# Softmax attention beside linear attention on one core: a new order for all five engines, and 76 of VectorE's score groups that add their second exponential pattern by an accumulating transfer

## The chip, the cores and the metric

The kernel runs on one core of one Trainium2 chip. The metric is the device time of one execution in microseconds (us). The core has five engines with queues of their own: TensorE (PE, matmuls into PSUM, which has eight banks of 128 x 512 float32), VectorE (DVE), ScalarE (ACT), GpSimd (POOL) and SyncE (SP, which here issues transfers only). SP, ACT and POOL can each issue transfers (DMAs); the page names such queues SPq, ACTq and POOLq. PEld is the loading of weights into TensorE.

## The reference

The input x has 2048 rows of 512 columns; there are 32 heads of 16. Branch A is linear attention with a softmax feature map, branch B is softmax attention, and a gate mixes the two:

```
g = sigmoid((x * gate_w).sum(-1, keepdims=True))
A:  phi(p) = concat(softmax(p), softmax(-p)),  p = q @ w_phi  or  k @ w_phi
    o = (phi_q @ (phi_k^T v)) / (phi_q . sum(phi_k) + 1e-6);   a = o @ wo
B:  p = softmax(q k^T / 4);   b = (p v) @ wo
return g * a + (1 - g) * b
```

Nearly all the work is in branch B: 32 heads x 2048 x 2048 scores, each of which goes through an exponential.

## The kernel before

**Tiles and units of work.** A tile is a 128 x 512 block of scores: 128 keys of one head by 512 queries. Four heads at a time make a quad of four tiles, and there are 512 quads (32 blocks of 16; a block is 8 heads' even or odd half against 512 queries). TensorE writes a tile into one PSUM bank (L892, one matmul that uses 32 rows of the array). Then the exponential is made by one of two engines:

- ScalarE takes 324 quads: one ACTIVATE with Exp reads two tiles, now and then three or one (L975), and writes bf16 into a ring of 24 tiles, E_t. One round of four matmuls (L903) then multiplies the four tiles by the values and adds them into the block's bank of sums.
- VectorE takes 188 quads, called groups: `add_group`. It adds a constant to the scores and writes them as 16-bit integers whose bits, read as bf16, are a coarse exponential (L938; L933 where two tiles go in one instruction, "pairs"). That is the first pattern, in a buffer t. GpSimd adds 35 to each 16-bit number (INT64_ADD on four at a time, L919, operation s) and writes a second buffer s; later it adds 48 more in place (operation m). The three patterns together approximate the exponential. In this kernel each gives a round of four matmuls on TensorE: `ps` (pattern two, from s), `pt` (pattern one, from t) and `pm` (pattern three, from s after m).

A group has a fourth number, `acc`, that is 0 for all of them here. With `acc` 1 the round `ps` is not made; instead GpSimd issues a transfer that adds buffer s onto buffer t in on-chip memory (L948), and `pt` waits for it:

```
if acc:
    op = P.add("pool", lambda e: e.dma_start(quarters(t), quarters(s), accum_op=ALU.add), reads=[s], ...)
else:
    ops.append(add_round(quad, part(s), [s], f"ps.{n}"))
ops.append(add_round(quad, part(t), [(t, i) for i in range(4)], f"pt.{n}"))
ops.append(shifted(n, s, s, STEPS[1] - STEPS[0], "m"))
ops.append(add_round(quad, part(s), [s], f"pm.{n}"))
```

A buffer is 128 x 2048 bf16, 512 KB. Operation m writes s, so it waits for that transfer too. The buffers are a pool of tiles that are free in that stage of the program: Tx_t, Ty_t, Tz_t, WoA_t, WoB_t, oT_t and phiQT_t from the start, WAT_t, vA_t, Wp_t and WB_t once the weights in them are used up.

**Small transfers.** When a block's sums are complete, its division goes over a chain of small DMAs on SP: Tf_t to memory (ld, L1018), back in another shape (Lq, L1020), VectorE's reciprocal, out (lr, L1027), back as a broadcast (Rb_t, eight DMAs, L1029), beside a merge of Tf_t (four DMAs, L1023). New queries need two sets of four small DMAs on qz_t (L850, L852).

**Branch A for queries** runs in four steps of 512 queries between the tiles of branch B. ScalarE makes the exponentials EA_t, VectorE scales them, SP writes them to memory (`pw`, L1247, dpq<-EA_t). SP then issues eight transposing transfers back (`Tq`, L1253: four into phiQT_t, four into WAT_t). They wait for the four writes and, for the first step, for the last use of phiQT_t as a group buffer. TensorE's denominators (`Z`, L1265) wait for all eight; numerators (`N`, L1278) follow. EA_t has two halves, so TensorE's projection for a later 128 queries (`P0`, L709) waits for the write of an earlier one.

**What sets the order.** Each engine executes its queue in order, and a waiting instruction holds all behind it. `TABLE` lists, for every engine, the numbers of its operations in the order in which they are issued, besides the split of quads between ScalarE and VectorE (`acts`, `groups`), the tiles of each Exp (`sizes`), the PSUM bank of each fill (`homes`) and the pairs (`pairs`). The semaphore waits are derived from the data that each operation reads and writes. `WENG` names the queue that loads each part of the weights of branch B.

Of the kernel before, what the change touches and what calls it, by code (L numbers as in the profile page):

```python
# [34 lines left out]
WENG = ("sp", "pool", "sp", "sp", "sp", "sp")  # L35
TABLE = {
    "acts": [
# [11 lines left out]
    "sizes": (  # L49
        "32332323322222221222212222222222222222222222222222222222222222222222222222222222222222222222222222332222222222222222222222222222222322222232"  # L50
        "22222222222222222222222222222222222222222222222222223232222222222222222222222222222222222222222222222222222222222222222222222222222222222222"
        "22222222222222222222232322222222222222222222222222222222222222222222222222222222222222222223222221222222222222222222222222222222222222222222"
        "22222222222222222222222222222222222222222222222222222222222222222222222222222222222222222222222222222222222222222222222222222222222222222222"
        "2222222222222222222222222222222222222222222222222222222222222222222222222223132122"),
    "groups": [
# [508 lines left out]
def _build(ctx, nc, A_x, A_wqkv, A_w_phi, A_wo, B_wqkv, B_wo, gate_w, out, table):  # L564
# [81 lines left out]
    for i, (nm, o, n) in enumerate((("wbk0", D, 128), ("wbq0", 0, 128), ("wbv0", 2 * D, 128),  # L646
                                    ("wbq", 128, 384), ("wbk", D + 128, 384), ("wbv", 2 * D + 128, 384))):
        dma(WENG[i], lambda e, o=o, n=n: e.dma_start(W_B[:, :, o:o + n], wb_v[:, :, o:o + n]), [nm], name=nm)
    for rr in range(8):
# [754 lines left out]
```

## Time and profile before

| | |
|---|---|
| median of 2 runs | 695.08 us (695.07 to 695.09) |
| the profiled execution | 696.42 us |
| its span, first to last instruction | 694.6 us |
| mean granted TensorE clock | 0.979 |
| bytes moved by DMAs | 30.93 MB |

The profile is of one execution; its busy times, counts and waits all belong to the 694.6 us. In views by window, each engine's busy time is followed by its number of instructions in brackets, then the granted TensorE clock as a share of full speed, the busy share of the DMA engines and what they moved. In timelines a row gives start and duration in us, the engine, the line and the tiles; in square brackets stands the idle time before it and what ended it.

### The profile page before, as it was taken

What the parts mean: (1) busy time and instruction counts of PE and PEld (TensorE: products, weight loads), DVE (VectorE), ACT (ScalarE), POOL (GpSimd) and SP (SyncE); (2) the same over time, 40 slices, a digit from 0 to 9 for tenths busy, and PEclk for the clock granted to TensorE, in tenths of its full rate; (3) what the DMA queues carried; (4) which work ended last, traced back from release to release, by engine and by line L of the source; (5) the groups of instructions that cost most, each with busy time, mean ns of one, the idle gap of its engine ahead of it and who ended that gap; (6) DMA issues with size and microseconds to landing.
All of it is one profiled execution on the core that took longest, in us unless ns stands there. A gap on an engine that the chain in (4) does not pass through costs nothing.

```text
span 694.6 us, 20402 instructions
## 1 busy us (share of the span) xinstructions
PE 673.4 (97%) x8759; PEld 231.6 (33%) x8759; DVE 627.4 (90%) x955; ACT 645.6 (93%) x713; POOL 408.2 (59%) x418
## 2 busy tenths in 40 slices
PE   7999999999999999999998999999999999999997
PEld 4433334343333342323332332322333323222222
DVE  6898897988988989999996899899999998999996
ACT  3999999999999999999996899899999998999993
POOL 4474534554546536697745567463676636875785
PEclk9999999999999999999997899899999999999999
DMA  9011100101000000010203115231232241111120
GB/s 221 6 37 35 36 21 15 25 3 36 5 11 22 1 20 18 17 52 10 59 18 95 27 37 123 57 89 30 71 88 89 56 97 31 54 36 28 30 43 32
DMA packets 62522, 30.93 MB, mean 45 GB/s; under 512 B 46216, under 2 KB 57352, under 8 KB 62432
## 3 DMA queue, kind: packets, MB, share of 16 engines
q1 hardware_dynamic: 61424, 28.95, 17.2%
q8 instruction: 69, 1.13, 0.7%
q10 hardware_dynamic: 576, 0.52, 0.2%
q0 software_dynamic: 432, 0.15, 0.1%
q14 instruction: 21, 0.17, 0.1%
HBM read 9.44 MB, written 8.88 MB: 26 GB/s over the span
## 4 chain that ended last, share of the span: by engine, by line
PE 73%; DVE 14%; SPq 4%; ACT 3%; DMA 3%; issue 2%; POOL 1%; DVEq 0%
PE ps L892 27%; PE ps L903 26%; PE ps L709 13%; SPq L1253 3%; ACT E_t L975 3%; PE ps L1182 2%; DVE vA_t L938 2%; DVE vA_t L933 1%; PE ps L795 1%; DVE oT_t L1032 1%; PE ps L808 1%; DMA WAT_t<-dpq 1%; DVE Tz_t L938 1%; DVE oT_t L938 1%; PE ps L1278 1%
## 5 line engine op out<-in xcount | busy, mean ns | idle before, releaser
L975 ACT ACTIVATE E_t<-ps 128x1024 bf16<-128x1024 f32 (+1 forms) x642 | 613.8, 1043 | 33.2 <-PE ps L892 29.2
L892 PE MATMUL ps<-qz_t,kTB_t 32*128 32x512 bf16 x2048 | 287.9, 389 | 7.1 <-DVE vA_t L938 1.4
L892 PEld LDWEIGHTS ps<-qz_t,kTB_t 32*128 32x128 bf16 x2048 | 74.5, 91 | 242.4 <-ACT E_t L975 117.9
L903 PE MATMUL ps<-E_t,vaug_t 128*32 128x512 bf16 (+1 forms) x1296 | 122.7, 388 | 0.1
L938 DVE TENSOR_SCALAR oT_t<-ps 128x512 int16<-128x512 f32 x128 | 84.1, 683 | 5.1 <-PE ps L892 4.6
L919 POOL INT64_ADD Tx_t<-Tx_t x45 | 47.2, 1050 | 43.1 <-PE ps L903 43.0
L938 DVE TENSOR_SCALAR vA_t<-ps 128x512 int16<-128x512 f32 x104 | 68.3, 681 | 2.7 <-PE ps L892 2.2
L919 POOL INT64_ADD vA_t<-vA_t x49 | 51.2, 1048 | 29.3 <-PE ps L903 16.5
L919 POOL INT64_ADD Ty_t<-Ty_t x42 | 43.6, 1040 | 22.5 <-PE ps L903 18.1
L903 PEld LDWEIGHTS ps<-E_t,vaug_t 128*32 128x32 bf16 (+1 forms) x1296 | 32.1, 95 | 47.4 <-issue 38.6
L938 DVE TENSOR_SCALAR phiQT_t<-ps 128x512 int16<-128x512 f32 x60 | 40.6, 686 | 5.9 <-PE ps L892 5.4
L709 PE MATMUL ps<-Wp_t,xT_t 128*32 128x512 bf16 x512 | 42.5, 390 | 3.1 <-DMA dpq<-EA_t 3.0
L903 PE MATMUL ps<-vA_t,vaug_t 128*32 128x512 bf16 x464 | 45.1, 389 | 0.4 <-POOL vA_t L919 0.4
L903 PE MATMUL ps<-Ty_t,vaug_t 128*32 128x512 bf16 x388 | 38.6, 390 | 0.4 <-POOL Ty_t L919 0.4
L903 PE MATMUL ps<-Tx_t,vaug_t 128*32 128x512 bf16 x388 | 38.4, 391 | 0.0
L709 PE MATMUL ps<-xT_t,WB_t 128*32 128x512 bf16 x480 | 37.5, 383 | 0.6 <-DVE Ty_t L933 0.6
L938 DVE TENSOR_SCALAR WoB_t<-ps 128x512 int16<-128x512 f32 x50 | 33.0, 684 | 5.0 <-PE ps L892 4.5
L938 DVE TENSOR_SCALAR WoA_t<-ps 128x512 int16<-128x512 f32 x52 | 34.4, 685 | 3.0 <-PE ps L892 2.7
L938 DVE TENSOR_SCALAR Ty_t<-ps 128x512 int16<-128x512 f32 x50 | 33.0, 681 | 1.8 <-PE ps L892 1.5
L938 DVE TENSOR_SCALAR Wp_t<-ps 128x512 int16<-128x512 f32 x46 | 30.3, 684 | 2.5 <-PE ps L892 2.0
L933 DVE TENSOR_SCALAR vA_t<-ps 128x1024 int16<-128x1024 f32 x24 | 29.2, 1221 | 1.6 <-PE ps L892 1.5
L938 DVE TENSOR_SCALAR Tx_t<-ps 128x512 int16<-128x512 f32 x44 | 29.0, 682 | 1.3 <-PE ps L892 1.1
(207 smaller groups left out, 992.6 us busy)
## 6 DMA issues: line engine op xcount, KB each, us to landing
dpq<-EA_t SPq DMA_DIRECT2D x16, 256.0 KB, 2.2
Rb_t<-lr SPq DMA_DIRECT2D x120, 32.0 KB, 1.8
dpo<-kv_t SPq DMA_DIRECT2D x16, 128.0 KB, 1.8
qz_t<-qz_t SPq DMA_DIRECT2D x120, 16.0 KB, 1.8
Tf_t<-Tf_t SPq DMA_DIRECT2D x60, 32.0 KB, 2.0
phiK_t<-in_A_x_dram SPq DMA_DIRECT2D x3, 512.0 KB, 8.0
WB_t<-in_B_wqkv_dram SPq DMA_DIRECT2D x3, 384.0 KB, 4.5
out_dram<-WvA_t SPq DMA_DIRECT2D x8, 128.0 KB, 1.9
```

Of the source, the lines that this page charges most:

```text
L709: ins = e.matmul(out[32 * i:32 * i + 32, :], lhsT=lhsT[:, 32 * i:32 * i + 32], rhs=rhs, start=start, stop=stop, tile_position=(0, 32 * i))
L795: mms = [lambda e, ap, i=i, t=t: e.matmul(ap[:, 128 * i:128 * (i + 1)], lhsT=xT[:, t, NQ * c + 128 * i:NQ * c + 128 * (i + 1)], rhs=W_B[:, ...
L808: mms = [lambda e, ap, i=i, t=t: e.matmul(ap[:, 256 * i:256 * (i + 1)], lhsT=xT[:, t, NQ * c + 128 * (2 * hf + i):NQ * c + 128 * (2 * hf + ...
L892: op = P.add("pe", lambda e: e.matmul(f.ap(), lhsT=kT_B[32 * i:32 * i + 32, ROW[b // 2] % 2, 128 * kt:128 * (kt + 1)], rhs=qz[32 * i:32 * ...
L903: return e.matmul(P.sums[b].ap()[32 * i:32 * i + w, :], lhsT=vaug[:, kt, o:o + w], rhs=rhs, start=start, stop=stop, tile_position=(0, 32 * ...
L919: op = P.add("pool", lambda e: e.int64_add(quarters(dst).bitcast(I64), quarters(src).bitcast(I64), step * 0x0001000100010001), reads=[(src ...
L933: return e.tensor_scalar(quarters(t)[:, a[0]:a[1] + 1:a[1] - a[0], :].bitcast(I16), ps3[:, c[0]:c[1] + 1:c[1] - c[0], :], EXPB, 0.0, op0=A ...
L938: d = P.add("dve", lambda e, i=i, f=f: e.tensor_scalar(quarters(t)[:, group.places.index(i), :].bitcast(I16), f.ap(), EXPB, 0.0, op0=ALU.a ...
L975: return e.activation(Ebuf[:, 512 * k:512 * (k + n)].rearrange("p (a c) -> p a c", c=512), ps3[:, where[0]:where[-1] + 1:step, :], ACTF.Ex ...
L1032: P.add("dve", lambda e: e.tensor_tensor(oT[:, r, qc, :], Tf[:, 0, :], Rb[:], ALU.mult), reads=[("Tf", 0), "Rb"], writes=[("oT", qc, r)], ...
L1182: mms = [lambda e, ap, n=n, f=f: e.matmul(ap[:, 64 * n:64 * n + 64].rearrange("p (s g j) -> p s g j", s=2, j=4), lhsT=ident[:], rhs=es[n][ ...
L1253: turned(f"Tq{n % 2}", [lambda e, g=g: e.dma_start_transpose(qT(g), dpq[n % 2, :, 128 * g:128 * (g + 1)]) for g in range(8)], [("dpq", n % ...
```

## The change

Only numbers change. ScalarE gets 322 quads in place of 324, VectorE 190 groups in place of 188; 76 of these groups (numbers 0 to 3 of every ten) have `acc` 1. So the rounds of four matmuls with the values go from 324 + 3 x 188 = 888 to 322 + 3 x 190 - 76 = 816, and GpSimd issues 76 accumulating transfers of 512 KB. ScalarE's Exp instructions go from 642 (620 of two tiles, 17 of three, 5 of one) to 641 (623, 12, 6); the pairs from 71 to 67. One weight load, 128 KB for the first queries, moves from GpSimd's queue to ScalarE's. The order of all five queues and the banks are new throughout.

```diff
-WENG = ("sp", "pool", "sp", "sp", "sp", "sp")
+WENG = ("sp", "act", "sp", "sp", "sp", "sp")
...
-        (3, "woA", "x0", 0), (19, "woB", "x1", 0), (7, "o2", "y0", 0), (15, "o3", "y1", 0), (14, "pt", "z", 0), (31, "woA", "woB", 0), (30, "o2", "x0", 0),
...
+        (3, "woA", "x0", 1), (19, "woB", "x1", 1), (11, "o2", "y0", 1), (10, "o3", "y1", 1), (15, "pt", "z", 0), (31, "woA", "x0", 0), (30, "pt", "y0", 0),
...
```

Three places are shown as they stand in the engines' queues. Names: ISA is GpSimd's INT64_ADD; a number such as x8 counts instructions of one kind that follow each other.

GpSimd's queue, before, about a tenth into the program, where groups 20 to 22 get their first shift:

```order
L919 ISA Ty_t<-phiQT_t 128x1024
L1161 CAST vA_t<-stat_t 128x16x4
L919 ISA Tx_t<-Tx_t 128x1024
L704 COPY mask_t<-mask_t 128x64
L919 ISA Tx_t<-WoA_t 128x1024
L919 ISA WoB_t<-WoB_t 128x1024
L919 ISA Tz_t<-oT_t 128x1024
```

The same groups now, with their accumulating transfers (L948):

```order
L919 ISA Tz_t<-phiQT_t 128x1024
L919 ISA Tx_t<-Tx_t 128x1024
L948 DMA phiQT_t<-Tz_t 128x2048
L919 ISA Ty_t<-oT_t 128x1024
L948 DMA oT_t<-Ty_t 128x2048
L919 ISA Tx_t<-Tx_t 128x1024
L919 ISA oT_t<-WoA_t 128x1024
L948 DMA WoA_t<-oT_t 128x2048
L919 ISA Tz_t<-Tz_t 128x1024
```

Each transfer stands one or two rows behind the shift that fills its source; the next in-place shift of that source (here Tz_t<-Tz_t) stands some rows later and has to wait for it.

SP's queue, before, at the first set of transposes of branch A's queries:

```order
L1018 DMA ld<-Tf_t 4x512
L1247 DMA dpq<-EA_t 128x1024
L1253 DMA_TRANSPOSE phiQT_t<-dpq 128x512 x4
L1018 DMA ld<-Tf_t 4x512
L1253 DMA_TRANSPOSE WAT_t<-dpq 128x512
L1247 DMA dpq<-EA_t 128x1024
L1020 DMA Lq_t<-ld 128x16
L1253 DMA_TRANSPOSE WAT_t<-dpq 128x512
L1020 DMA Lq_t<-ld 128x16
L1247 DMA dpq<-EA_t 128x1024
L1253 DMA_TRANSPOSE WAT_t<-dpq 128x512 x2
L850 DMA qz_t<-qz_t 16x512 x4
```

The same place now:

```order
L1018 DMA ld<-Tf_t 4x512
L1253 DMA_TRANSPOSE phiQT_t<-dpq 128x512 x4
L850 DMA qz_t<-qz_t 16x512 x4
L1253 DMA_TRANSPOSE WAT_t<-dpq 128x512 x4
L1018 DMA ld<-Tf_t 4x512
L1020 DMA Lq_t<-ld 128x16 x2
L1023 DMA Tf_t<-Tf_t 16x512 x4
L1247 DMA dpq<-EA_t 128x1024
L1287 DMA dpo<-kv_t 128x512 x2
```

The two writes of EA_t (L1247) that stood between the transposes stand behind them, and four DMAs on qz_t stand between the first four transposes and the last four.

TensorE's queue, before, ahead of the denominators (L1265) that wait for these transposes:

```order
L709 MATMUL ps<-Wp_t,xT_t 32x512 x8
L892 MATMUL ps<-qz_t,kTB_t 128x512 x3
L709 MATMUL ps<-Wp_t,xT_t 32x512 x4
L892 MATMUL ps<-qz_t,kTB_t 128x512 x3
L709 MATMUL ps<-Wp_t,xT_t 32x512 x4
L903 MATMUL ps<-E_t,vaug_t 32x512 x8
L892 MATMUL ps<-qz_t,kTB_t 128x512 x2
L903 MATMUL ps<-Ty_t,vaug_t 32x512 x4
L1265 MATMUL ps<-kzbd_t,phiQT_t 128x4 x4
```

The same place now:

```order
L1182 MATMUL ps<-EA_t,ident_t 128x64 x16
L892 MATMUL ps<-qz_t,kTB_t 128x512 x4
L903 MATMUL ps<-vA_t,vaug_t 32x512 x4
L892 MATMUL ps<-qz_t,kTB_t 128x512 x3
L903 MATMUL ps<-E_t,vaug_t 32x512 x4
L892 MATMUL ps<-qz_t,kTB_t 128x512 x2
L903 MATMUL ps<-E_t,vaug_t 32x512 x4
L903 MATMUL ps<-vA_t,vaug_t 32x512 x4
L892 MATMUL ps<-qz_t,kTB_t 128x512 x4
L1265 MATMUL ps<-kzbd_t,phiQT_t 128x4 x4
```

The round that releases the transposes (the last use of phiQT_t's group, a round on Tx_t) stands 41 rows and 44 tiles (L892) ahead of the denominators before, 17 rows and 22 tiles ahead now.

More of the change, by code (lines that the diff above doesn't have):

```diff
@@ L34 @@
 XACT = (1,)
-WENG = ("sp", "pool", "sp", "sp", "sp", "sp")
+WENG = ("sp", "act", "sp", "sp", "sp", "sp")
 TABLE = {
     "acts": [
[11 rows of a table removed]
[11 rows of a table added]
     "sizes": (
-        "32332323322222221222212222222222222222222222222222222222222222222222222222222222222222222222222222332222222222222222222222222222222322222232"
-        "22222222222222222222222222222222222222222222222222223232222222222222222222222222222222222222222222222222222222222222222222222222222222222222"
-        "22222222222222222222232322222222222222222222222222222222222222222222222222222222222222222223222221222222222222222222222222222222222222222222"
+        "22222222222222222222222222222222222222222222222222222222222222222222222222222222222222222222222222222222222222222322222122222232223222222222"
+        "22223222222222122222222222222222322212222223322222232323222212222222222222222222222222222222222222222222222222222222222222232222222212222222"
@@ L53 @@
         "22222222222222222222222222222222222222222222222222222222222222222222222222222222222222222222222222222222222222222222222222222222222222222222"
-        "2222222222222222222222222222222222222222222222222222222222222222222222222223132122"),
+        "22222222222222222222222222222222222222222222222222222222222222222222222222222222222222222222222222222222222222222222222222222222222222222222"
+        "222222222222222222222222222222222222222222222222222222222222222222222222222222231"),
     "groups": [
[42 rows of a table removed]
@@ L98 @@
-    "act": [
[171 rows of a table removed]
-    "dve": [
[38 rows of a table removed]
-    "pool": [
[17 rows of a table removed]
-    "homes": (
-        "01675061320713245074653420173546731207365420126457021345672613745671253472153467512476412576452147561247621457645214567412756241705640214567"
-        "05412706241570641256075214607412074602416704210721063421064321026340513465104230516243056124356104321654231516063250163250162637016571037650"
-        "13675130467301567403165710374531067645310635476304157640316473017641034761023674012467120476102764105276501267401526745106742051467501421706"
-        "52410645231645341245162356124365217653471245317263451275432614357651243712503465143261052435210435023143152032154210543126354120463512064351"
-        "02546701324716403712036401643206342160423610324610234016234012637016732140327610423570143524103275035217340125340521053421504235140235342013"
-        "45012473015637451046370517364150437601547361034617560435706134071634671034107613407064320213461240352143650123540154612306450321546013254630"
-        "21465032451632615426341052630176327051326710563725103276501763201573265107325716045273601734501324615042310653420162354016453062153426403215"
-        "46320451237654132675413276541673245132675142631745623741573217625436713247650314257621345673214756352164571237645342157642154327614231673421"
-        "67432706121346074130627134046712347201674320174361206437123401270364215746301264531206534023146521036541025642016531043562301654201546312045"
-        "61027465021467510256705214506721504762450217645062175041265431270357412604735162743651234576124536712354217654326175347163254167324576324563"
-        "42657043027652306750426305476230456320654023540637240572350473125407231054712304530124532701542730514327514027530145327041235410536201562530"
-        "41523104524360123416023401654326521306541230456214356120356012536021465321057630145673410756410346534760134765103674105473650163470371426573"
-        "42651437215674312564371256437125342136475216437251673421574351027603416720134267013426710346720134672013462701346270341627341204751264507126"
-        "34571234560132740412371504237401537205142375410237407134207125437014532701327605432706132517063256107231506732105267351032760152367051326014"
-        "52360451623405136201453260154623451063210543245106423710643257107243501732541073250143274051732541034271057234501327601253061532671062310765"
-        "23170523710523601576235103276150327160572130561325106237105436204516235140623140523610456231045236051423654016325014632541023541072435017314"
-        "250154230532404523540263"),
@@ L345 @@
-    "pairs": [
[7 rows of a table removed]
[42 rows of a table added]
+    "act": [
[168 rows of a table added]
+    "dve": [
[38 rows of a table added]
+    "pool": [
[20 rows of a table added]
+    "homes": (
+        "10216013254013274321065237140265307154602173540126435201754632106432015324506132450163425601432601532451043620514326104653270156437106345107"
+        "64531760543671053461705437061574361054375013746510726341052673051673201567230513627051623507126537012365107623570152735601762301562315026350"
+        "14362451026305142631045326140523615406321064532175463126453127567412345673126457231741235761423764532164521365436215461253421654021603457215"
+        "34271653472154376541327653142562134562154312654231745603217560231475623104653214052360415324104354201354012354061423501652341063246104723564"
+        "32746572346532675234674327563217653426517436125637412357641275643211546713265431562754201654012654015346021534620153415026154005461205462106"
+        "45310264351063451204357210534102321040514231045201435107354021435210754320153427134523417561347561435764307651304653041571603475610754371053"
+        "46170634570154360173465103475106345106423016534210652345601243061324502164356731204650312654213654310234561024531206453012643523016543160542"
+        "16054236104563240123710423761407263410623706142376104273670132674201365132754607234105632104362450132601456203415024531602430615420356145320"
+        "61523610426310473260143627401672314037261407632014632704127346017326710630124367201563471026501342615023420136540214536210654321065431025302"
+        "41536412056310352671035621073562701256723061572365107235017236501627301567421304762107436120347602143670261374601437240127346013274106723610"
+        "73267013270613267053120632017563021756301265310276302516371056327031647342061742307614203160217346017204317623014671032746210346732103672140"
+        "34760314673071653741564371506143075614307563416750431675134576341056427351042375107534201354072105472013540213540321745021374501274350127340"
+        "51273541207541674522067541276405672045126745167245162751407625104276310476531402671430762314670423160743217063214706123604713024760234216701"
+        "23076132507612307623106723116570327516302156021306531720651273650712453624015623410562341063521043465021645021465320165341206541023640152634"
+        "50613461703462013674102673420163470167340167234107263701463520146235145036245016324015236501423650142365012345610234261043560214356012543601"
+        "23640176423170432706134207613246071034712037416203476210543671452317634257165234156724356723476541327645132765214356723417651234765342567032"
+        "576324657243576342634314"),
```

566 rows, old and new, of the table TABLE are left out of this document.

## The prediction

> **What bounds the kernel now.** First the page: its span, the engines' busy times, the granted clock in 40 slices, the costliest groups.
>
> ```profile
> span 694.6 us, 20402 instructions
> PE 673.4 (97%) x8759; PEld 231.6 (33%) x8759; DVE 627.4 (90%) x955; ACT 645.6 (93%) x713; POOL 408.2 (59%) x418
> PEclk9999999999999999999997899899999999999999
> L919 POOL INT64_ADD Tx_t<-Tx_t x45 | 47.2, 1050 | 43.1 <-PE ps L903 43.0
> L938 DVE TENSOR_SCALAR vA_t<-ps 128x512 int16<-128x512 f32 x104 | 68.3, 681 | 2.7 <-PE ps L892 2.2
> ```
>
> ScalarE is busy 93%, TensorE 97%, VectorE 90%: three engines near their limit, so the average decides nothing. Therefore next the view by windows, to see where ScalarE, which has the least room inside a stage, is idle. (Columns: length, busy time and instructions of PE, PEld, DVE, ACT and POOL, clock, DMA share, GB/s.)
>
> ```profile
> 0.00:20.00 20.00, 16.20 (x138) 9.21 (x139) 12.71 (x42) 9.17 (x10) 8.46 (x17) 0.91 0.79 191
> 20.00:350.00 330.00, 327.94 (x4461) 117.30 (x4463) 298.63 (x450) 321.83 (x359) 188.04 (x198) 1.00 0.10 23
> 350.00:400.00 50.00, 46.49 (x567) 14.88 (x556) 41.48 (x65) 42.79 (x50) 26.27 (x26) 0.86 0.20 49
> 400.00:450.00 50.00, 47.55 (x580) 16.43 (x576) 46.07 (x67) 46.29 (x52) 30.25 (x29) 0.93 0.28 69
> 450.00:550.00 100.00, 98.75 (x1299) 31.58 (x1296) 96.73 (x148) 97.92 (x111) 64.08 (x62) 1.00 0.28 72
> 550.00:600.00 50.00, 47.73 (x621) 14.93 (x613) 45.62 (x67) 46.00 (x51) 24.97 (x24) 0.97 0.30 69
> 600.00:680.00 80.00, 78.00 (x956) 23.21 (x952) 77.37 (x109) 78.43 (x85) 59.31 (x59) 1.00 0.14 32
> 680.00:694.60 14.60, 10.75 (x175) 4.08 (x171) 8.82 (x14) 3.13 (x4) 6.77 (x7) 0.96 0.12 38
> ```
>
> ScalarE's idle time is 10.8 us at the start, 8.2 in 20 to 350, 7.2 in 350 to 400, 3.7 in 400 to 450, 2.1, 4.0 in 550 to 600, 1.6, and 11.5 at the end: 49.1 in all. In 20 to 350 it is 97.5% busy. So span = ScalarE's work (645.6) + its idle time (49.1), and I forecast these two. Of the idle time 22.3 us are the ends; 14.9 lie in three stretches in which the clock falls. What happens in the first of them, in the timeline:
>
> ```profile
> 360.16 0.40 PE L903 MATMUL ps<-Tx_t,vaug_t 128*32 128x512 bf16 x4
> 360.60 5.09 SPq L1253 DMA_TRANSPOSE phiQT_t<-dpq  x4
> 371.05 0.43 SPq L1247 DMA_DIRECT2D dpq<-EA_t  x1
> 373.43 1.05 PE L709 MATMUL ps<-Wp_t,xT_t 128*32 128x512 bf16 x8 [2.97 <-DMA dpq<-EA_t]
> 374.03 2.48 SPq L850 DMA_DIRECT2D qz_t<-qz_t  x4
> 375.08 2.11 ACT L975 ACTIVATE E_t<-ps 128x1024 bf16<-128x1024 f32 x2 [3.52 <-PE ps L892]
> ```
>
> ```profile
> 370.00:375.00 5.00, 2.03 (x22) 0.40 (x18) 1.46 (x3) 1.56 (x2) 2.51 (x3) 0.75 0.52 134
> 375.00:380.00 5.00, 5.00 (x62) 1.70 (x60) 3.13 (x4) 3.48 (x5) 1.04 (x1) 0.50 0.18 36
> 380.00:385.00 5.00, 5.00 (x47) 1.36 (x44) 3.40 (x7) 3.64 (x4) 1.01 (x1) 0.50 0.29 58
> 385.00:390.00 5.00, 4.71 (x58) 1.45 (x55) 4.23 (x7) 4.27 (x5) 3.49 (x4) 0.89 0.18 58
> ```
>
> A small write of EA_t stood behind six transposes on SP's queue and landed at 373.4; TensorE waited 2.97 us for it, ScalarE 3.52. Then TensorE's clock stood at half until about 387, and ScalarE lost another 3.5 us (20 us less 12.95 busy, less 3.52). A wait of TensorE thus costs about twice its length here. The other two stretches are smaller cases of the same:
>
> ```profile
> 435.89 0.24 PE L1265 MATMUL ps<-kzbd_t,phiQT_t 128*128 128x4 bf16 x4 [0.58 <-DMA WAT_t<-dpq]
> 580.57 1.94 ACT L975 ACTIVATE E_t<-ps 128x1024 bf16<-128x1024 f32 x2 [1.05 <-PE ps L892]
> ```
>
> **The change part by part.** *ScalarE's work.* It makes three more Exp of two tiles, five fewer of three, one more of one tile.
>
> ```profile
> L975 ACT ACTIVATE E_t<-ps 128x1024 bf16<-128x1024 f32 x620 | 588.2, 1035 | 28.3 <-PE ps L892 24.5 <-PE ps L903 0.8
> L975 ACT ACTIVATE E_t<-ps 128x1536 bf16<-128x1536 f32 x17 | 24.7, 1459 | 5.0 <-PE ps L892 4.8
> ```
>
> 588.2/620 = 0.95 us for two tiles, 24.7/17 = 1.45 for three; 3 x 0.95 - 5 x 1.45 + at most 0.95 is -3.5 to -4.4. I take -4. VectorE gets eight more tiles at 0.66 (68.3/104), and four fewer pairs: +6 us on 627, covered by its own room of 67.
>
> *TensorE's rounds.* 888 - 816 = 72 fewer. Two rounds in a row start 0.22 us apart:
>
> ```profile
> 306.31 0.40 PE L903 MATMUL ps<-E_t,vaug_t 128*32 128x512 bf16 x4
> 306.53 0.39 PE L903 MATMUL ps<-vA_t,vaug_t 128*32 128x512 bf16 x4
> ```
>
> That is 15.8 us less of TensorE, but where ScalarE is 97 to 98% busy it only becomes waiting. At most it removes ScalarE's idle time outside ends and stretches, 8.2 + 2.1 + 1.6 = 11.9; at least nothing. TensorE's relief is 8% of its rounds and the waits have many causes: I take -3, range 0 to -8.
>
> *GpSimd's issues.* 76 accumulating transfers, one weight load less, two groups' shifts more.
>
> ```profile
> 1.25 0.92 POOL L648 DMA_DIRECT2D WB_t<-in_B_wqkv_dram  x1 [0.82 <-POOLq L1389]
> 9.11 0.58 POOL L693 DMA_DIRECT2D gw_t<-in_gate_w_dram  x1
> ```
>
> An issue takes 0.58 to 0.92 us; at 0.75, between them because a buffer has 128 long rows, that is 57 us, and with 4 x 1.05 for shifts GpSimd goes from 408 to about 469 of some 690. Its room hides it. Gone, it would show as later shifts.
>
> *The accumulating transfers' landing.* No row shows such a transfer. The nearest move the same 512 KB, from device memory, without adding:
>
> ```profile
> WoA_t<-in_A_wo_dram SPq DMA_DIRECT2D x1, 512.0 KB, 5.2
> WvA_t<-in_A_wqkv_dram SPq DMA_DIRECT2D x1, 512.0 KB, 3.9
> phiK_t<-in_A_x_dram SPq DMA_DIRECT2D x3, 512.0 KB, 8.0
> phiQT_t<-dpq SPq DMA_TRANSPOSE x16, 2.8
> ```
>
> So 3.9 to 8.0 us from issue to landing; I take 6, above the middle of the kernel's 5.2, because the sum is read as well as written. What it may take is read in TensorE's queue: between a group's last tile and its round on t stand 26 to 65 tiles, 40 in the median. The tiles go from the first Exp to the last:
>
> ```profile
> L975 ACT ACTIVATE E_t<-ps x642: 591/1025/1490, 13.1 to 683.1; 128x1024 bf16<-128x1024 f32 x157, 128x1536 bf16<-128x1536 f32 x3, 128x512 bf16<-128x512 f32 x1
> ```
>
> 2048 tiles in 670 us are 0.33 us each, so 8.6 to 21 us, 13 in the median. Of these 3.2 go to the tile (0.4), VectorE (0.7), the shift (1.05) and one instruction ahead of it on GpSimd (1.05). Summed over the 76 groups, landing at 5.2 us makes nobody late, 6 costs 0.6 us, 7 costs 5, 8 costs 17, 9 costs 39 (each late group counted with what its round waits). I take +1. [...]
>
> *The first transposes (350 to 400).* EA_t's writes no longer stand between them, so the 2.97 us wait goes. Next is the wait of L1265 for all eight transposes. They start with the round on Tx_t (360.16 to 360.60 before). From there: 8 issues at 1.27 (5.09/4), with four DMAs on qz_t (2.48) now between, less the last issue, plus landing 2.8: 0.44 + 7 x 1.27 + 2.48 + 2.8 = 14.6 us. TensorE needs for what stands before L1265, 22 tiles, about 6 us (before, 36 tiles took it from 360.70 to 370.46, 0.27 each); 6.5 with the sums L1182. It waits about 8 us. ScalarE loses about as much, and again 3.5 to the clock: 12 in place of 7.2. Term +5. Bounds: +7 (8.6 for the wait and the refill behind it, 3.5 to the clock, 2 if the round on Tx_t comes late), and -7 if it does not wait at all. Behind L1265 stand all later tiles, so ScalarE and VectorE wait with it.
>
> [...]
>
> *The other two stretches.* In SP's queue the second and third sets of transposes now have their broadcast (Rb_t, eight DMAs) behind them instead of ahead, the fourth has its writes of EA_t early. From the end of the block whose sums go out between them, a set needs VectorE's copy (about 1.7 with its turn), four merges (2.48), eight issues (10.2), three or four small ones at 0.43 and the landing (2.8): 18 to 19 us for the second and third; for the fourth, of which half is out by then, 11. TensorE has 68, 69 and 47 tiles ahead of the three L1265 from that point, at 0.27 to 0.33 us 18 to 22, 19 to 23 and 13 to 16 us. I expect no wait over 1 us: idle 3.7 falls to 1.4, 4.0 to 1.0, so -5.3; range -7 to +3, as 2 us of lateness of the small transfers bring the waits of the second and third back.
>
> *The ends.* Ahead of the first Exp TensorE now also does nearly all transposes of x: +1 (range -1 to +3). The weight load on ScalarE's queue is hidden by its waits for x. At the end as many rounds follow the last tile as before.
>
> Sum: -4 - 3 + 1 + 5 - 5.3 + 1 = -5.3. The profiled execution took 696.42 us for its span of 694.6; its counterpart would take 691.1. The median of the runs, 695.08, lies 1.34 below, so 689.8: I forecast **690**.
>
> **Rivals.** *As forecast*, one new wait of 8 us at L1265, two old ones gone: 690, own range 683 to 698. Chance 0.60.
>
> *Slower: the accumulating transfers land late.* At pt, from 8 us on: 16 groups, 17 us, in place of the 1 counted: 706; at 9 us 728. It is 709 from 8.2 us on. For it: 8.0 in the row of phiK_t, four such transfers within some 14 us, and waits that lower the clock. Against it: that row is from the crowded start (DMA share 0.79), later ones show 3.9 to 5.2. Chance of 709 or more 0.16.
>
> *Faster: the transposes are not waited for, and TensorE's relief counts.* Term -7 in place of +5, -6 in place of -3: 675; half of it gives 681. Against it: the 1.27 us per issue are the same in all four sets. Chance of 681 or less 0.10.
>
> *It does not help:* new waits eat what the old ones gave, 695 to 704. 0.5 us in each of the 19 bursts of four such transfers (9.5 us) would do, from small transfers that come late beside them. For it: in 550 to 600 us the small transfers and transposes alone already keep the DMA engines busy 0.30 of the time. Chance 0.14. [...]
>
> 2% of 695.08 is 13.9 us, about what a measurement can tell from no change: 681.2 and 709.0. Faster 0.10, same 0.74, slower 0.16. Range 679 to 715: below it lies most of the fast rival (0.07), above it the late transfers from some 8.4 us of landing on (0.12).
>
> **What would show it.** Right: L1265 waits 6 to 10 us near 365 with the clock at half behind it, no wait for EA_t's writes near 370 and 562, Exp x641, transfers of L948 landing in 5 to 7 us, few waits of L903 for them. Wrong: landing over 8 us with L903 waiting in most groups, or no wait at L1265.

## The result and the profile after

| | before | changed |
|---|---|---|
| median | 695.08 us | 750.61 us (two runs, 750.34 and 750.88) |
| ratio, 95% interval | | 1.080 [1.075, 1.085] |
| span of the profiled execution | 694.6 us | 748.5 us |
| ScalarE busy | 645.6 us | 641.4 us |
| ScalarE idle (span less busy) | 49.0 us | 107.1 us |

The change made the kernel 8.0% slower; forecast were 690 us, range 679 to 715. ScalarE's work fell by 4.2 us as forecast. Everything that was lost is idle time of ScalarE, 58 us more. In the experiments below one execution, 715.6 us with 38 transfers, was slower at a lower granted clock and is left out.

The page of the changed kernel: span, engines' busy times, clock in 40 slices, the queue that GpSimd issues into (packets, MB, share of 16 DMA engines), a group of shifts.

```profile
span 748.5 us, 19978 instructions
PE 683.6 (91%) x8471; PEld 229.4 (31%) x8471; DVE 635.9 (85%) x967; ACT 641.4 (86%) x712; POOL 488.7 (65%) x497
PEclk9999999999999999899959888999988997896999
q0 software_dynamic: 19392, 39.87, 30.9%
L919 POOL INT64_ADD Tx_t<-Tx_t x42 | 48.7, 1174 | 8.8 <-PE ps L903 6.5
```

TensorE has 72 rounds fewer and yet 10 us more busy time, as its granted clock falls again and again from 300 us on (0.83 to 0.93 in the windows below; 0.936 in the mean, 0.979 before). The accumulating transfers alone keep the 16 DMA engines busy 31% of the span. The shifts' rows are longer, 1.17 us in the mean where they were 1.05, but their pace is the same: in a run without a gap they end 1.0 us after one another in both kernels, only that a row often begins before the one ahead of it has ended. Where the time went is in the windows (columns as before: length, busy time of PE, PEld, DVE, ACT, POOL, clock, DMA share, GB/s):

```profile
0.00:20.00 20.00, 15.17 (x147) 9.68 (x148) 12.82 (x42) 5.28 (x7) 6.94 (x17) 0.91 0.95 194
20.00:300.00 280.00, 275.50 (x3765) 100.54 (x3762) 256.76 (x381) 272.98 (x310) 186.99 (x201) 1.00 0.39 76
300.00:350.00 50.00, 40.56 (x455) 11.65 (x453) 39.87 (x60) 39.57 (x45) 33.92 (x33) 0.93 0.49 96
350.00:400.00 50.00, 37.78 (x478) 12.62 (x479) 35.12 (x56) 35.88 (x40) 27.54 (x26) 0.83 0.50 84
400.00:450.00 50.00, 46.21 (x522) 13.84 (x519) 42.63 (x66) 43.20 (x50) 36.39 (x37) 0.90 0.69 141
450.00:550.00 100.00, 89.97 (x1070) 29.43 (x1068) 86.25 (x133) 84.54 (x94) 65.38 (x63) 0.91 0.55 104
550.00:600.00 50.00, 44.60 (x553) 13.94 (x551) 43.49 (x67) 42.98 (x49) 34.10 (x32) 0.93 0.48 103
600.00:680.00 80.00, 73.25 (x780) 20.52 (x779) 66.00 (x98) 68.36 (x73) 53.18 (x53) 0.87 0.61 106
680.00:748.50 68.50, 60.60 (x733) 17.22 (x725) 52.98 (x72) 48.57 (x52) 44.31 (x43) 0.90 0.42 81
```

Up to 300 us ScalarE is busy 272.98 of 280 us, no worse than before, with the DMA engines busy 39%. So accumulating transfers can be hidden: 32 of the 76 are issued there. Small ones go beside them, 40 of Rb_t's up to 290 us among them, and do land later, after up to 4.4 us where it was 3.3 before; but no wait for a transfer of SP's queue is recorded there. From 300 us on, where branch A's queries add their writes and transposes, ScalarE loses 7 to 14 of every 50 us. What such a loss looks like, in the timeline: SP's eight issues of a broadcast (lr to Rb_t), VectorE's product that waits for it, and ScalarE.

```profile
295.14 11.15 SPq L1029 DMA_DIRECT2D Rb_t<-lr  x8
302.01 0.68 DVE L938 TENSOR_SCALAR WoB_t<-ps 128x512 int16<-128x512 f32 x1
308.06 1.02 ACT L975 ACTIVATE E_t<-ps 128x1024 bf16<-128x1024 f32 x1 [3.13 <-PE ps L892]
309.07 0.72 DVE L1032 TENSOR_TENSOR oT_t<-Tf_t,Rb_t 128x512 bf16<-128x512 f32 x1 [6.38 <-DMA Rb_t<-lr]
312.76 1.02 ACT L975 ACTIVATE E_t<-ps 128x1024 bf16<-128x1024 f32 x1 [3.68 <-PE ps L892]
```

Eight issues take 11.15 us. The same eight take 3.82 us where the accumulating transfers are of 4 KB (second experiment). VectorE starts nothing between 302.7 and 309.07 us, so the tiles behind L1032 wait 6.38 us with it; ScalarE is idle 3.13 and 3.68. Of the waits of the whole kernel (us in total, times, longest), ScalarE's and the largest that end in a DMA:

```profile
ACT E_t L975 <- PE ps L892: 87.6, 83, 12.8
PE ps L1265 <- DMA WAT_t<-dpq: 15.6, 2, 12.0
DVE oT_t L1032 <- DMA Rb_t<-lr: 10.0, 4, 6.4
POOL WB_t L919 <- DMA Tx_t<-WB_t: 9.7, 3, 5.9
DVE rd_t L1025 <- DMA Lq_t<-ld: 8.9, 3, 4.2
PE ps L709 <- DMA dpq<-EA_t: 3.3, 2, 1.7
```

TensorE and VectorE wait for small transfers (Rb_t, Lq_t, dpq) and transposes, 37.8 us in these rows. For the accumulating ones TensorE's matmuls wait 4.8 us in the whole kernel and GpSimd, which has room, 24.1. Their landing is about what was forecast (L948, from issue to landing):

```profile
DMA to landing us min/median/max: 4.5/5.7/10.5
```

### The profile page after: what moved, and what is told of

It is laid out like the page before. It is cut to its first block, busy times and chain, and to the rows that moved or that the text cites. A ratio compares the mean times of both kernels' runs of the same rounds, so it can differ in the third digit from the quotient of the medians.

```text
span 748.5 us, 19978 instructions
## 1 busy us (share of the span) xinstructions
PE 683.6 (91%) x8471; PEld 229.4 (31%) x8471; DVE 635.9 (85%) x967; ACT 641.4 (86%) x712; POOL 488.7 (65%) x497
## 3 DMA queue, kind: packets, MB, share of 16 engines
q0 software_dynamic: 19392, 39.87, 30.9%
## 4 chain that ended last, share of the span: by engine, by line
PE 47%; DVE 18%; DMA 10%; SPq 8%; ACT 7%; POOL 6%; issue 2%; ACTq 0%; DVEq 0%; POOLq 0%
PE ps L892 17%; PE ps L903 16%; PE ps L709 10%; ACT E_t L975 7%; SPq L1029 3%; DMA Tx_t<-WB_t 2%; DVE vA_t L938 2%; DVE oT_t L1032 2%; SPq L1253 2%; DMA Lq_t<-ld 2%; DVE Tx_t L938 2%; PE ps L1182 2%; SPq L1023 1%; DMA vA_t<-Ty_t 1%; POOL Tx_t L919 1%
## 5 line engine op out<-in xcount | busy, mean ns | idle before, releaser
L892 PE MATMUL ps<-qz_t,kTB_t 32*128 32x512 bf16 x2048 | 298.5, 399 | 20.2 <-DVE vA_t L938 6.9
L892 PEld LDWEIGHTS ps<-qz_t,kTB_t 32*128 32x128 bf16 x2048 | 76.5, 91 | 260.8 <-ACT E_t L975 105.4
L903 PE MATMUL ps<-E_t,vaug_t 128*32 128x512 bf16 x1288 | 124.6, 402 | 0.0
L938 DVE TENSOR_SCALAR vA_t<-ps 128x512 int16<-128x512 f32 x114 | 74.3, 682 | 8.9 <-PE ps L892 8.4
L919 POOL INT64_ADD vA_t<-vA_t x51 | 58.2, 1142 | 35.1 <-PE ps L903 25.2
L938 DVE TENSOR_SCALAR oT_t<-ps 128x512 int16<-128x512 f32 x114 | 74.9, 682 | 7.0 <-PE ps L892 6.4
L938 DVE TENSOR_SCALAR Tx_t<-ps 128x512 int16<-128x512 f32 x64 | 41.6, 680 | 9.0 <-PE ps L892 8.9
L903 PEld LDWEIGHTS ps<-E_t,vaug_t 128*32 128x32 bf16 x1288 | 31.8, 97 | 47.0 <-issue 40.0
L938 DVE TENSOR_SCALAR phiQT_t<-ps 128x512 int16<-128x512 f32 x52 | 33.8, 683 | 4.2 <-PE ps L892 4.2
L1032 DVE TENSOR_TENSOR oT_t<-Tf_t,Rb_t 128x512 bf16<-128x512 f32 x15 | 20.9, 1393 | 10.0 <-DMA Rb_t<-lr 10.0
L919 POOL INT64_ADD Ty_t<-oT_t x13 | 14.8, 1142 | 18.3 <-DVE oT_t L938 18.3
```

Of the source, the lines that this page charges most:

```text
L892: op = P.add("pe", lambda e: e.matmul(f.ap(), lhsT=kT_B[32 * i:32 * i + 32, ROW[b // 2] % 2, 128 * kt:128 * (kt + 1)], rhs=qz[32 * i:32 * ...
L903: return e.matmul(P.sums[b].ap()[32 * i:32 * i + w, :], lhsT=vaug[:, kt, o:o + w], rhs=rhs, start=start, stop=stop, tile_position=(0, 32 * ...
L919: op = P.add("pool", lambda e: e.int64_add(quarters(dst).bitcast(I64), quarters(src).bitcast(I64), step * 0x0001000100010001), reads=[(src ...
L938: d = P.add("dve", lambda e, i=i, f=f: e.tensor_scalar(quarters(t)[:, group.places.index(i), :].bitcast(I16), f.ap(), EXPB, 0.0, op0=ALU.a ...
L1032: P.add("dve", lambda e: e.tensor_tensor(oT[:, r, qc, :], Tf[:, 0, :], Rb[:], ALU.mult), reads=[("Tf", 0), "Rb"], writes=[("oT", qc, r)], ...
```

## The experiments

Each run stands beside runs of the kernel before on the same chip; those took 695.1 us beside the changed kernel, and 698.3, 696.6 and 696.2 in the three sets below. So kernels of different sets are compared by their ratios.

**The order alone.** In the table, the last number of 75 groups is 0, and the 75 transfers leave GpSimd's list and become rounds in TensorE's (one group, whose third round opens its block's sums, keeps its transfer).

```diff
-        (3, "woA", "x0", 1), (19, "woB", "x1", 1), (11, "o2", "y0", 1), (10, "o3", "y1", 1), (15, "pt", "z", 0), (31, "woA", "x0", 0),
+        (3, "woA", "x0", 0), (19, "woB", "x1", 0), (11, "o2", "y0", 0), (10, "o3", "y1", 0), (15, "pt", "z", 0), (31, "woA", "x0", 0),
...
```

> The changed order on all engines, but 75 of the 76 accumulating transfers become rounds of TensorE again (each some 16 of TensorE's instructions ahead of the group's third or last round). Theory A, the transfers are what costs (they, and the small transfers that come late beside them): the time falls to between 690 and 705 us, that is to the kernel before and up to 10 us above it for 75 rounds of 0.22 us on TensorE; the small transfers' issues on SP's queue go back to 2.4 us for four, and L1032 waits for Rb_t less than 3 us in all. Theory B, the new order itself costs: the time stays above 735 us.

716.5 us, ratio 1.025 [1.018, 1.032]. Between the two: the transfers cost most, but the order itself costs 2.5%, with as many rounds on TensorE as before (891 against 888), 75 more than it was made for. ScalarE is idle 71.5 us; Rb_t's landing is back at 1.8 us in the median.

**Transfers of 4 KB, and transfers that copy.** Two runs that keep the changed order and all 76 issues:

```diff
-            op = P.add("pool", lambda e: e.dma_start(quarters(t), quarters(s), accum_op=ALU.add), reads=[s],
+            op = P.add("pool", lambda e: e.dma_start(quarters(t)[:, 0, 0:16], quarters(s)[:, 0, 0:16], accum_op=ALU.add), reads=[s],
```

```diff
-            op = P.add("pool", lambda e: e.dma_start(quarters(t), quarters(s), accum_op=ALU.add), reads=[s],
+            op = P.add("pool", lambda e: e.dma_start(quarters(t), quarters(s)), reads=[s],
```

> The changed kernel, but each accumulating transfer moves 16 columns of one quarter of the buffer in place of 2048 columns (4 KB in place of 512 KB); the output leaves out most of the second pattern in these 76 groups. Issues, waits and order stay. Theory A1, it is the volume (the 512 KB share the DMA engines with the small transfers and land late): 690 to 705 us, landing about 2 to 3 us. Theory A2, it is the issue on GpSimd and the fixed part of a transfer: 725 to 750 us. Theory B, the order: above 735 us.

> The changed kernel, but the 76 transfers copy their 512 KB without adding; the output leaves out the first pattern in these 76 groups. If adding is what makes them slow (the sum must be read as well as written), they land in 3.5 to 4.5 us and the time falls to 700 to 720 us. If the volume and the place beside the small transfers count, landing stays over 5 us and the time within 740 to 755 us.

711.3 us, ratio 1.018 [1.005, 1.031], with 4 KB; 711.4 us, 1.018 [1.012, 1.024], with 512 KB copied without adding. The first is above the 705 us that were expected of it, so order and issues cost something of their own; the second is as the first of its two theories said. Copies of 512 KB thus cost nothing that these intervals can tell from transfers of 4 KB. It is the adding that costs: 1.080 against 1.018. With 4 KB the eight issues of Rb_t that took 11.15 us stand so in the timeline:

```profile
293.33 3.82 SPq L1029 DMA_DIRECT2D Rb_t<-lr  x8
```

Of the copying kernel, the page's row of GpSimd's queue, and the landing of L948:

```profile
q0 software_dynamic: 11328, 39.87, 15.4%
```

```profile
DMA to landing us min/median/max: 2.9/3.6/7.5
```

The same 39.87 MB take half the DMA engines' time (15.4% against 30.9%) and land in 3.6 us in place of 5.7.

**Long rows.** Wp_t and WB_t are laid out so that each of their buffers is 128 rows of 4 KB rather than 512 of 1 KB.

```diff
-    Wp = sb([128, KT, 2 * D], name="Wp")
+    Wp = sb([128, 2, KT, D], name="Wp")
-    W_B = sb([128, KT, 3 * D], name="WB")
+    W_B = sb([128, 3, KT, D], name="WB")
...
```

> The changed kernel, with Wp_t and WB_t laid out with each used buffer as 128 rows of 4 KB in place of 512 rows of 1 KB; nothing else differs and nothing is left out. Theory S, the buffers of 512 short rows are what lands late (7 to 10 us from 290 us on): their issue falls from 1.3 to 1.7 us to 0.87, their landing to 5 to 6 us, and the time by at least 15 us, to 735 us or less. Theory A1, all 512 KB transfers alike disturb the small ones: the time falls by less than 8 us, to 743 us or more.

743.7 us, ratio 1.064 [1.049, 1.079] against 1.080 [1.075, 1.085]. That lies between the two theories, and the intervals overlap. The transfers with these buffers do land earlier (Tx_t from WB_t in 7.7 us in place of 10.1), but that is not the main cost: ScalarE is still idle 98.4 us.

**Traffic that nobody waits for.** The rounds and shifts no longer wait for a transfer, but the DMA engines stay busy. Once with plain copies of 1 MB within device memory (junk_v is half of B_x, which the kernel does not read; junk has a place for each group), once with transfers that add 512 KB from xT_t to device memory:

```diff
-            op = P.add("pool", lambda e: e.dma_start(quarters(t), quarters(s), accum_op=ALU.add), reads=[s],
-                       writes=[(t, i) for i in range(4)], name=f"acc.{n}", sem=acc_sems[t][0])
+            op = P.add("pool", lambda e: e.dma_start(junk[n], junk_v), name=f"acc.{n}", sem=acc_sems[t][0])
...
-            ops.append(op)
```

```diff
+            op = P.add("pool", lambda e: e.dma_start(junk[n], xT[:, 0, :], accum_op=ALU.add), reads=xk0, name=f"acc.{n}", sem=acc_sems[t][0])
```

> The changed kernel, but each of the 76 accumulating transfers is replaced by a plain copy of 1 MB between two places in device memory, issued by GpSimd at the same place of its order and waited for by nobody; the output leaves out the second pattern in these 76 groups. It keeps the DMA engines about as busy as the accumulating transfers (share 0.31), but nothing waits for its landing. Theory I, the transfers cost by making the small transfers late: 735 to 755 us, with Rb_t, Lq_t and the transposes as late as in the changed kernel. Theory L, they cost because their own rounds, and GpSimd's shifts behind them, wait for their landing: 705 to 718 us, as with 4 KB.

> The changed kernel, but each of the 76 transfers adds 512 KB (128 rows of 4 KB, from xT_t) to a place of its own in device memory, and nobody waits for its landing; the output leaves out the second pattern in these 76 groups. Issue, rows, bytes and adding stay as in the changed kernel, the wait for the landing goes. Theory I, the adding transfers cost by making the small transfers late: 735 to 755 us. Theory L, they cost because their own rounds and shifts wait for them: 705 to 718 us. A time between tells the two shares.

The copies: 795.8 us, ratio 1.142 [1.136, 1.148], beyond both expectations. The adds: 734.3 us, 1.054 [1.047, 1.062], just below the first theory's band and far above the second's. In the copies' kernel the wait for Rb_t (view of waits) has grown from 10.0 to 34.2 us:

```profile
DVE oT_t L1032 <- DMA Rb_t<-lr: 34.2, 9, 7.7
```

and the adds' kernel, whose queue is busy 32.3%, still has these, though no instruction waits for an adding transfer:

```profile
ACT E_t L975 <- PE ps L892: 72.9, 68, 11.6
PE ps L1265 <- DMA WAT_t<-dpq: 15.2, 3, 10.7
DVE oT_t L1032 <- DMA Rb_t<-lr: 5.7, 2, 5.4
```

In the kernel with 4 KB the first two are 49.8 and 8.8, and there is no wait for Rb_t. So the small transfers, late beside the large ones, cost without anybody waiting for the large ones. The copies show that share of DMA time is not the measure by itself: at 28.9% they hurt much more than the adds at 32.3%. They move twice the bytes, in rows of 8 KB in place of 4; whether that or device memory at both ends does it was not tried.

**VectorE held by GpSimd.** In the kernel with 4 KB, two waits of 4.68 and 4.00 us of ScalarE remained, at 309 and 344, though no small transfer was late. The timeline of that kernel, VectorE's product and GpSimd's shifts at the first:

```profile
300.19 0.68 DVE L938 TENSOR_SCALAR WoB_t<-ps 128x512 int16<-128x512 f32 x1
300.79 5.13 DVE L1032 TENSOR_TENSOR oT_t<-Tf_t,Rb_t 128x512 bf16<-128x512 f32 x1
...
299.65 1.69 POOL L919 INT64_ADD WAT_t<-WAT_t  x1
300.66 1.68 POOL L919 INT64_ADD Ty_t<-Ty_t  x1
301.68 2.68 POOL L919 INT64_ADD vA_t<-vA_t  x2
303.70 1.66 POOL L919 INT64_ADD Ty_t<-Ty_t  x1
308.73 1.04 POOL L919 INT64_ADD vA_t<-WoB_t  x1 [3.37 <-DVE WoB_t L938]
```

L1032 takes 0.68 us in its fastest executions. Here it takes 5.13 and ends half a microsecond after GpSimd's run of shifts. A run without a gap does not do that by itself. In the kernel before, L1208, whose two inputs lie in on-chip memory too, meets a run of seven shifts that lasts to 298 us, and takes 0.92 us:

```profile
291.12 0.92 DVE L1208 TENSOR_TENSOR EA_t<-EA_t,ratio_t 128x512 bf16<-128x512 bf16 x1
291.48 1.46 POOL L919 INT64_ADD Wp_t<-oT_t  x1
```

What the long one has besides is a transfer that GpSimd issued 3.8 us before it (the last section comes back to this). Three added waits of GpSimd let such operations through:

```diff
+    called = {op.name: op for op in P.ops}
+    for a, b in (("s.75", "T2.11"), ("s.85", "phi0.3.1"), ("m.123", "T2.19")):
+        called[a].deps = called[a].deps + [called[b]]
```

> The kernel with transfers of 4 KB (most of the second pattern left out in 76 groups), with three added waits of GpSimd: a shift waits for VectorE's L1032 of the block pair that ran 5.13 us at 301, one for the L1208 that ran 4.18 us at 336, one for the L1032 of 2.70 us at 485. Theory P, VectorE's two-input operations cannot go on while GpSimd works without a pause: the three take at most 2.2, 2 and 2 us, ScalarE's waits of 4.68 us (309) and 4.00 us (344) go, and the time falls by 8 to 13 us from 711 to between 698 and 703 us. If something else holds VectorE there, they stay at 3 us or more and the time above 708 us.

699.7 us, ratio 1.003 [1.000, 1.006], against 1.018 [1.005, 1.031], as expected, though the intervals just meet; the profiled executions differ by 6.5 us (706.0, 699.5). The same place:

```profile
301.75 2.13 DVE L1032 TENSOR_TENSOR oT_t<-Tf_t,Rb_t 128x512 bf16<-128x512 f32 x1
...
301.64 1.68 POOL L919 INT64_ADD Ty_t<-Ty_t  x1
303.98 2.05 POOL L919 INT64_ADD vA_t<-vA_t  x2 [0.65 <-DVE oT_t L1032]
```

GpSimd pauses 0.65 us, VectorE is through after 2.13 us, and ScalarE's two waits shrink to 0.79 and 0.98 us. Part of the gain is given back: another L1032, which took 1.46 us at 645 without the breaks, now meets a run of shifts.

```profile
634.13 5.72 DVE L1032 TENSOR_TENSOR oT_t<-Tf_t,Rb_t 128x512 bf16<-128x512 f32 x1
```

**The first transposes, earlier.** They waited for all work of the groups that use phiQT_t, also for the rounds on those groups' other buffers. Now they wait only for what touches phiQT_t. This was tried on the kernel before and on the kernel with 4 KB and breaks.

```diff
-            op.deps = op.deps + wp_ops + users["pt"]
+            op.deps = op.deps + wp_ops + P.readers["pt"] + [x for i in range(4) for x in P.readers[("pt", i)] + P.writer[("pt", i)]]
```

> The kernel before, in which the first transposes wait only for the last work that touches phiQT_t (the shift and the round of group 87), no longer for the rounds on the other buffers of its groups. They can start some 8 us earlier, at about 352 in place of 360.6 us. If the waits in the stretch 350 to 400 hang on that start, EA_t's write at 371 goes out earlier, the wait of 2.97 us and the half clock behind it go, and the time falls by 4 to 8 us, to a ratio of 0.988 to 0.994. If not, the ratio is 0.997 to 1.003.

> As the run with three breaks (transfers of 4 KB, most of the second pattern left out), and the first transposes wait only for the last work that touches phiQT_t, so that they start some 14 us earlier. Theory: the wait of L1265 (9 us) and its half clock go, 10 to 13 us less than the run with breaks alone: 686 to 692 us. That would leave of the new order's cost only the start of the kernel (3 us). If the transposes' start is not what L1265 waits for: within 3 us of the run with breaks alone.

On the kernel before: 691.5 us, ratio 0.993 [0.991, 0.996]: 0.7%, 4.7 us, of the 7 us of idle time that the forecast read in 350 to 400. This kernel is faster than both. On the other: 688.5 us, 0.988 [0.984, 0.993]. In the stretch 350 to 400, without and with it, ScalarE (fourth) is busy 39.22 and 47.94 us:

```profile
350.00:400.00 50.00, 40.61 (x506) 13.20 (x502) 39.26 (x62) 39.22 (x46) 28.62 (x29) 0.90 0.30 65
```

```profile
350.00:400.00 50.00, 48.03 (x622) 16.24 (x614) 49.40 (x76) 47.94 (x55) 36.37 (x38) 0.99 0.40 80
```

**The repairs together, and half the transfers.** The changed kernel, nothing left out, with long rows, early transposes and four breaks; and the same with every second transfer turned back into a round.

```diff
+    for a, b in (("s.75", "T2.11"), ("s.85", "phi0.3.1"), ("m.123", "T2.19"), ("s.173", "T2.27")):
...
```

> The changed kernel with nothing left out, and the repairs of the earlier runs together: buffers of 128 long rows, four waits of GpSimd that let VectorE's two-input operations through (the three before, and one for the L1032 that ran 4.01 us at 672), and the first transposes as early as phiQT_t allows. If the repairs add up: 743.7 - 11.6 for the breaks and - 11.2 for the transposes - about 5 for the fourth break, 716 to 722 us, a ratio of about 1.03. If the adding transfers bring other waits in their place: 728 us or more.

> As the repaired kernel, with nothing left out, but only every second of the 76 groups uses its accumulating transfer; the other 38 add by a round of TensorE. If the adding transfers' cost is in proportion to their number, it lies half way between the repaired kernel and one with none (716 for the order alone, less some 9 for early transposes, 707): 710 to 715 us. If four in a burst are what hurts, two in a burst cost little and the time is 700 to 707 us.

737.2 us, ratio 1.058 [1.052, 1.065]: the repairs do not add up, and the second alternative holds. Breaks and early transposes are worth some 20 us with transfers of 4 KB (1.018 to 0.988) and, beside long rows (1.064), hardly anything with full ones. L1265 still waits 9.5 us in all for its transposes (14.5 without the repairs), L1032 11.3 for Rb_t, L1025 8.1 for Lq_t: with small transfers late everywhere, a stall taken away is followed by the next late one. With 38 transfers 706.8 us, 1.011 [1.003, 1.018], at the upper end of the second expectation, and too wide to tell whether the number of transfers or their coming in fours counts. L1032 then waits 1.8 us for Rb_t.

**One more on the kernel before.** With early transposes VectorE waited 2.36 us for Rb_t at 383, behind four transfers of qz_t on SP's queue that are needed 60 us later. They go behind the broadcast; in SP's queue:

```diff
-L850 DMA qz_t11<-qz_t11 16x512 x4
 L1027 DMA lr<-rd_t25 128x2x16
 L1023 DMA Tf_t24<-Tf_t24 16x512 x4
 L1029 DMA Rb_t27<-lr 16x512 x8
+L850 DMA qz_t11<-qz_t11 16x512 x4
```

> The kernel before with the early transposes, and on SP's queue four small transfers of qz_t (needed some 60 us later) moved from ahead of the broadcast Rb_t at 371 us to behind it. In the run with early transposes VectorE waits 2.36 us for that broadcast at 383, with half clock behind it. If that wait is the queue's: it goes, and the ratio falls from 0.993 to between 0.986 and 0.990. If not: 0.992 to 0.995.

690.3 us, ratio 0.991 [0.987, 0.995], just short of what was expected. The wait is gone from the timeline (early transposes alone, then with the move):

```profile
383.25 0.97 DVE L1032 TENSOR_TENSOR oT_t<-Tf_t,Rb_t 128x512 bf16<-128x512 f32 x1 [2.36 <-DMA Rb_t<-lr]
```

```profile
380.18 0.69 DVE L1032 TENSOR_TENSOR oT_t<-Tf_t,Rb_t 128x512 bf16<-128x512 f32 x1
```

Whether it is faster than early transposes alone (0.993) the intervals do not tell. Both beat the kernel before and the changed one.

## Why the prediction was wrong

ScalarE's idle time in the profiled executions, read step by step, splits the 58 us: order and issues with transfers of 4 KB +20 (68.8 against 49.0); the adding traffic without any wait for it +24 (92.4); waiting for the landing, with the 512 short rows, +15 (107.1, and 98.4 with long rows). By the ratios the three steps are 12, 25 and 18 us. The split is rough: two executions of one kernel lie up to 9.5 us apart, and the unwaited adds go to device memory, not to the buffers. Point by point:

- *ScalarE's work, -4*: right, 645.6 to 641.4.
- *TensorE's relief, -3*: at most a small gain over the kernel before. In 20 to 300 us ScalarE is busy 272.98 us after, 272.41 before, 274.55 with transfers of 4 KB. The new order needs it, though: with 75 rounds back (first experiment) ScalarE is idle 15.9 us in this stretch, against 7.0.
- *GpSimd's issues, 0, "its room hides it"*: **wrong.** The issues themselves are hidden (0.9 us in the median, 79.5 us for the 76 in place of 57). But runs of shifts that follow an issue can hold VectorE's two-input operations, of which the kernel before had none over 1.57 us. In the kernel with 4 KB that was worth 6.5 us by the profiled executions and 1.5 points, some 10 us, by the ratios; in the changed kernel L1032 took 4.93 us at 680 and 2.21 at 496. GpSimd's room (65% busy in the changed kernel) says nothing about how long VectorE's operations take beside its shifts (L1032 5.13 us with 4 KB, 0.68 at its fastest).
- *The accumulating transfers' landing, +1*: **the step that failed.** The duration was right, 5.7 us against 6, with a longer upper end (10.5 against 8.0); copies of the same 512 KB landed in 3.6 us (2.9 at least, the adds 4.5), so adding put about 2 us on a transfer. But the term counted only the rounds that wait for these transfers. The 31% of the DMA engines' time that 76 adds of 512 KB take, twice that of copies, was not a term. The rival "it does not help" had the mechanism, small transfers that come late beside them, at 0.5 us a burst and 0.14; its 9.5 us are some 24 by the trace with unwaited adds, 1.2 us a burst.
- *The first transposes, +5*: nearly right. Without adding traffic L1265 waits 8.8 us (forecast 8), and ScalarE is idle 11.4 us in 350 to 400 (forecast 12). In the changed kernel it is 12.0 and 14.1, because the first four transposes take 8.21 us to issue, not 5.09.
- *The other two stretches, -5.3*: wrong, in the main by the same cause. Idle went from 3.7 to 6.8 and from 4.0 to 7.0, where 1.4 and 1.0 were forecast. With 4 KB it was 4.4 and 1.8, so the term would have been -1.5 even without the adding; why the stretch from 400 to 450 did not gain there stays open. In the changed kernel the forecast's own condition for that, "2 us of lateness of the small transfers", was met: VectorE waits 4.2 us for one Lq_t. (The windows cover somewhat earlier work in the slower kernel.)
- *The ends, +1*: +3.9 at the start (idle 14.7 of the first 20 us, 10.8 before) and -1.0 in the last 14.6 us (10.5 against 11.5), at the upper end of its range. (In the rivals, half of the fast one's 15 us gives 682, not 681, which changes nothing here.)

## What to carry to other kernels

A transfer has two prices: what waits for it, and what comes late beside it (here about +15 and +24 us of ScalarE's idle time). Before putting bulk traffic beside a kernel that lives on many small transfers, take the small ones' issue and landing times and ask what the kernel does when they double; a stretch in which nothing waited for the small ones (here 20 to 300 us, ScalarE busy 272.98 us, 272.41 before) took the bulk free of charge, and those in which engines wait for them did not (7 to 14 of every 50 us). An engine with room to spare can still hold up a neighbour (here L1032 took 5.13 us beside GpSimd's shifts, 0.68 at its fastest): look for the neighbour's operations that last much longer than their shortest while the other engine works without a pause, and break the run there. And a wait for "all work of a group" is worth narrowing to the work on the one buffer: on the kernel before, that gave 0.7%.

## What the runs showed that was not expected

- Adding in a transfer doubles the DMA engines' time for the same bytes: 30.9% against 15.4% of the span, landing 5.7 against 3.6 us, issue on GpSimd 0.90 against 0.56 us in the median.
- SP's issues slow down beside such traffic, not only the landings: Rb_t's 120 issues take 56.7 us in all before, 57.6 beside transfers of 4 KB, 64.2 beside copies, 64.4 beside the unwaited adds to device memory, 78.4 in the changed kernel.
- GpSimd's shifts have longer rows after the issue of an adding transfer, whatever its size: 104 of 380 are over 1.2 us in the changed kernel and 112 with 4 KB, against 15 before and 15 with copies. They do not come more slowly for it: each row begins 0.3 to 0.7 us before the last one ends, and the ends stay 1.0 us apart.
- With 4 KB, VectorE's L1032 at 300.79 us, an operation of two inputs, took 5.13 us beside five shifts of GpSimd that started 1 us apart without a gap (299.65 to 305.36), and ended 0.56 us after the last of them; with a pause of 0.65 us in that run it took 2.13. All ten two-input operations of 3.8 us and more, in seven of the kernels here, began 0.7 to 3.8 us after GpSimd had issued a transfer. Where its last issue lay 4 us back or more, none took over 2.2 us, though one of them met seven shifts in a row. An issue shortly before is not enough either: the L1032 of 1.46 us at 645 in the kernel with 4 KB stood 2.1 us behind one. What else makes the difference stays open.
